# Seven block products for eight in the first product of a second MLP

## The chip, the cores and the metric

The kernel runs on one core of a Trainium2 chip (trn2). The metric is the device time of one execution in microseconds (us), as a median over runs. The engines are named as the profile names them: PE (TensorE matmul), PEld (its weight loads), DVE (VectorE), ACT (ScalarE), POOL (GpSimd), SP (SyncE, which starts the DMAs).

## What is computed

Causal attention with a window of 64 positions (4 batches, 8 heads, 576 positions, head size 64), then two MLPs on the 2304 tokens of width 512. All of it in float32:

```python
x = attn_out.transpose(0, 2, 1, 3).reshape(2304, 512)
h = x @ w_in                       # 512 -> 2048
x = (h * tanh(softplus(h))) @ w_out
h = x @ w_in2                      # 512 -> 1024: the first product of the second MLP
e = exp(h - h.max(-1)); sm = e / (e.sum(-1) + 1e-9)
solu = h * sm
ln = (solu - solu.mean(-1)) / sqrt(solu.var(-1) + 1e-6) * g_ln
return ln @ w_out2                 # 1024 -> 512
```

## The kernel before

Every float32 operand of a large product is split into a high half that PE takes exactly (rounded, type fp32r) and a low half (the value less the high half), and a product is three matmuls: high x high, high x low, low x high. `round_12` makes a high half, `rest` (L304) a low half; the engine is an argument.

The tokens go through attention and the first MLP in five groups of 512, 512, 512, 384 and 384. In the first MLP an iteration takes one of 16 slices of 128 hidden units: 12 matmuls into PSUM (`pe_m1`, L742), the activation on ACT (`act_m`, L752), its high half `g` (mostly ACT, L288) and low half (DVE, L308), then 8 matmuls on the high half (`pe_m2`, L776) and 4 on the low half (`pe_m2l`, L787), added up in four banks over the 16 slices. Attention of the next group runs beside it. The result goes to DRAM (`x2d`).

The second MLP takes the tokens in 18 tiles of 128. For each tile: `b_load` (L850) fetches it, transposed, as four blocks of 128 of the 512 inputs; `b_split` (ACT, L855) and `b_rest` (POOL, L860) make its halves; `b_m3` (L870) is 24 matmuls (4 blocks x 3 terms x 2 halves of the 1024 outputs) into the two banks of `h`; `b_max` (DVE, L877), `b_exp` (ACT, L883), `b_stat` (DVE, L889 on: h times exp, then mean and variance), `b_var` (POOL), `b_z` (DVE, L910 and L911) make the normed row; `b_tr` (L918) is 8 transposes; `b_hi` (ACT) and `b_lo` (DVE) split it; `b_m4` (L943) is 24 matmuls of the second product, `b_out` and `b_store` bring it out.

The weights arrive as float64 bits and are made float32 on the chip, piece by piece (`convert`): `c_up`, `c_low` (ACT or POOL), `c_bits`, `c_sign` (DVE), then `c_hi` and `c_lo`. Finished halves lie in buffers of two rings of four, `w1` and `w2`; the four pieces of `w_in2` (called w3) and those of `w_out2` (w4) take the buffers of the first MLP's weights as these come free, in its last group.

Nothing of this is in a fixed order in the code. Each piece of work is a `step` with its engines and assumed costs (`COSTS`), what it follows, what buffers it uses, and a due time; `Schedule.run` lays the steps out one by one, on each engine the one with the earliest due time among those that could start about now, and calls the functions in that order. So the order of instructions on each engine is what the tables of due times (`PRE_AT`, `ATT_AT`, `B_AT` and others, L50 to L69) make of it, and the engines then keep that order. Where a step of PE in the first part would stand idle for over 0.8 us by these costs, `bridge` (L518) fills the gap with small matmuls on zeros.

Of the kernel before, what the change touches and what calls it, by code (L numbers as in the profile page):

```python
# [24 lines left out]
P = 128  # L25
# [30 lines left out]
B_AT = (9.587, 37.912, -19.559, -30.209, 0.809, 34.651, 64.819, 43.703)

CONV_PRIO = (43.465, 59.161, 15.699, 11.465, 9.993, -9.387)
Q_LEAD = 1.101
V_LEAD = -62.18  # L60
G_AT = 1.058
K0_LATER = -88.806
FIRST_AT = (-161.938, -95.173, -8.712)
W_STEP = 0.88
M4_LATER = -28.799
BESIDE_AT = ((12.83, 25.285), (5.132, 29.901), (-14.786, 53.657), (-18.384, 60.677), (13.158, 1.338))
BESIDE_PE = 15.387
PATIENCE = 0.35
SLACK = 7.152  # L69
# [127 lines left out]
def attention_moe_solu(  # L197
# [624 lines left out]
    with tc.manual_schedule():  # L822
# [9 lines left out]
        def open_b():  # L832
            tctx.close()
            B["x"] = ctx.enter_context(tc.tile_pool(name="bx", bufs=2, side="right", reuse_waits="tile"))
            B["s"] = ctx.enter_context(tc.tile_pool(name="bs", bufs=4, side="right", reuse_waits="tile"))
            B["h0"] = ctx.enter_context(tc.tile_pool(name="pb_h0", bufs=1, space=PSUM, side="right", reuse_waits="tile"))
            B["mhalf"] = B["s"].tile([P, 1], F32, name="mhalf", bufs=1)
            nc.vector.memset(B["mhalf"], -0.5)

        def open_b2():  # L840
# [4 lines left out]
            B["h1"] = ctx.enter_context(tc.tile_pool(name="pb_h1", bufs=1, space=PSUM, reuse_waits="tile"))  # L845

        def b_load(t):
            j, o = tile_of[t]
            xr[t] = B["x"].tile([P, KD, P], F32, tag="xr", name="xr", bufs=1)
            nc.sync.dma_start(out=xr[t], in_=x2d[j][:, :, o:o + P])  # L850

        def b_split(t):
            r = xr.pop(t)
            xs[t] = B["x"].tile([P, 2, KD, P], F32R, tag="xs", name="xs", bufs=2)
            nc.scalar.activation(out=xs[t][:, 0], in_=r, func=ACTF.Copy)  # L855
            xr[t] = r

        def b_rest(t):
            r = xr.pop(t)
            nc.gpsimd.tensor_tensor(out=xs[t][:, 1], in0=r, in1=xs[t][:, 0].bitcast(F32), op=ALU.subtract)  # L860

        def b_m3(t):
            h2[t] = B["h" + str(t % 2)].tile([P, 2, 512], F32, tag="h2", name="h2")
            x = xs.pop(t)
            assert all(("w3", c, k) in split_done for c in range(2) for k in range(KD))

            terms = [(k, a, b) for k in range(KD) for a, b in ((0, 1), (0, 0), (1, 0))]
            for idx, (k, a, b) in enumerate(terms):
                for c in range(2):
# [387 lines left out]
```

## Time and profile before

| | |
|---|---|
| median of 3 runs | 704.94 us (704.12 to 705.28) |
| profiled execution | 706.97 us |
| its span (first to last instruction) | 705.1 us |
| busy share: PE, DVE, ACT, POOL | 99%, 54%, 44%, 8% |
| mean granted clock of PE, as a share of 2.4 GHz | 0.998 |

The span is what the trace covers; the profiled execution is 1.9 us longer than it, and 2.0 us above the median. Ends of matmuls are modelled in the records, each reaching into the next, so the spacing of matmuls is read from starts. An engine that is idle costs nothing unless the chain of waits runs through it.

### The profile page before, as it was taken

The page shows a single profiled execution, that of the slowest core. Times are in us where ns is not written, and L with a number is a line of the kernel's source. Part 1 is how long each engine was busy: PE and PEld are TensorE (multiplying, and loading weights), DVE is VectorE, ACT ScalarE, POOL GpSimd, SP SyncE. Part 2 cuts the span into 40 slices and gives each one's busy share as a digit, 9 for nine tenths or more (in the row PEclk, how much of TensorE's full clock was granted, in tenths as well). Part 3 has the DMA queues.
Part 4 walks back from the last instruction along what each step waited for, and adds up shares of the span by engine and source line. Part 5 has one row for each costly group of instructions (what it writes and reads, how often), then busy time and mean ns, then how long its engine had stood idle before and what let it go on. Part 6 is the DMA issues. An engine that isn't in the chain of part 4 may idle for free.

```text
span 705.1 us, 10722 instructions
## 1 busy us (share of the span) xinstructions
PE 695.4 (99%) x4429; PEld 597.2 (85%) x4429; DVE 382.0 (54%) x559; ACT 312.1 (44%) x536; POOL 56.9 (8%) x80
## 2 busy tenths in 40 slices
PE   9989999999999999999999999999999999999997
PEld 7779888888888888878899999999888888888886
DVE  4988776775662121656614114666766556565550
ACT  5769977475442222454534325663322222222231
POOL 2111000010000000000001100001122212111000
PEclk9999999999999999999999999999999999999999
DMA  8747355846213030323150105330111111110011
GB/s 288 296 156 293 121 178 179 278 160 219 90 46 106 0 119 31 119 91 120 31 165 1 31 1 165 120 119 32 44 59 46 46 45 46 46 45 31 16 45 46
DMA packets 37856, 71.74 MB, mean 102 GB/s; under 512 B 2864, under 2 KB 15152, under 8 KB 37808
## 3 DMA queue, kind: packets, MB, share of 16 engines
q1 hardware_dynamic: 37808, 71.06, 29.9%
q8 instruction: 35, 0.57, 0.3%
q14 instruction: 13, 0.11, 0.0%
HBM read 59.51 MB, written 11.53 MB: 101 GB/s over the span
## 4 chain that ended last, share of the span: by engine, by line
PE 94%; DVE 3%; DMA 2%; ACT 1%; issue 0%; SPq 0%; ACTq 0%
PE ps_h L742 27%; PE x L776 18%; PE h L870 14%; PE po L943 14%; PE x L787 9%; PE ps_o L696 2%; PE pt L918 2%; PE ps_t L659 2%; PE ps_s L564 2%; PE ps_w L516 1%; DMA st<-w_in 1%; DMA room_kv<-v 1%; PE ps_s L546 1%; DVE w L308 0%; DVE g L308 0%; DVE su L633 0%
## 5 line engine op out<-in xcount | busy, mean ns | idle before, releaser
L742 PE MATMUL ps_h<-xt,w 128*128 128x512 f32 (+2 forms) x1008 | 212.3, 361 | 0.3 <-ACT mc L752 0.2
L742 PEld LDWEIGHTS ps_h<-xt,w 128*128 128x128 f32 x1008 | 178.1, 189 | 22.9 <-issue 1.0
L776 PE MATMUL x<-g,w 128*128 128x512 f32 (+2 forms) x672 | 147.9, 362 | 0.0
L776 PEld LDWEIGHTS x<-g,w 128*128 128x128 f32 x672 | 118.1, 188 | 14.6 <-issue 0.9
L308 DVE SCALAR_TENSOR_TENSOR g<-mc,g 128x512 fp32r<-128x512 f32 (+2 forms) x84 | 53.2, 635 | 117.5 <-ACT g L288 117.0
L870 PE MATMUL h<-w,xs 128*128 128x512 f32 x432 | 104.0, 396 | 0.0
L943 PE MATMUL po<-w,lz 128*128 128x512 f32 x432 | 102.8, 394 | 0.0
L870 PEld LDWEIGHTS h<-w,xs 128*128 128x128 f32 x432 | 80.9, 188 | 19.0
L943 PEld LDWEIGHTS po<-w,lz 128*128 128x128 f32 x432 | 80.0, 188 | 16.3
L288 ACT ACTIVATE g<-mc 128x512 fp32r<-128x512 f32 (+2 forms) x70 | 39.8, 572 | 97.9 <-PE x L787 97.5
L787 PE MATMUL x<-g,w 128*128 128x512 f32 (+2 forms) x336 | 81.2, 363 | 0.0
L752 ACT ACTIVATE mc<-ps_h 128x512 f32<-128x512 f32 (+2 forms) x84 | 44.6, 535 | 78.1 <-PE ps_h L742 64.3
L787 PEld LDWEIGHTS x<-g,w 128*128 128x128 f32 x336 | 59.1, 188 | 7.1 <-issue 0.5
L924 ACT ACTIVATE lz<-pt 128x512 fp32r<-128x512 f32 x36 | 19.6, 596 | 63.2 <-PE po L943 49.5
L877 DVE TENSOR_REDUCE nm<-h 128x1 f32<-128x1024 f32 x18 | 22.0, 1224 | 45.8 <-PE h L870 45.8
L647 POOL TENSOR_TENSOR s<-s,rs 128x1024 f32<-128x1024 f32 x7 | 13.5, 1934 | 348.8 <-DVE rs L641 342.8
L368 DVE SCALAR_TENSOR_TENSOR st<-st 128x1024 uint32<-128x1024 uint32 x22 | 26.9, 1224 | 25.5 <-ACT st L360 25.5
L855 ACT ACTIVATE xs<-xr 128x512 fp32r<-128x512 f32 x18 | 11.4, 632 | 59.7 <-issue 32.2
L860 POOL TENSOR_TENSOR xs<-xr,xs 128x512 fp32r<-128x512 f32 x18 | 23.3, 1293 | 167.6 <-ACT xs L855 167.6
L889 DVE TENSOR_TENSOR y<-h,y 128x1024 f32<-128x1024 f32 x18 | 22.0, 1223 | 14.5 <-ACT y L883 14.5
L928 DVE TENSOR_TENSOR lz<-pt,lz 128x512 fp32r<-128x512 f32 x36 | 23.3, 686 | 12.2 <-ACT lz L924 11.0
L353 ACT ACTIVATE st<-st 128x1024 f32<-128x1024 f32 x22 | 25.3, 1149 | 9.5 <-DMA st<-w_in 6.4
(102 smaller groups left out, 651.7 us busy)
## 6 DMA issues: line engine op xcount, KB each, us to landing
qk<-qk SPq DMA_DIRECT2D x32, 512.0 KB, 5.0
st<-w_out SPq DMA_DIRECT2D x12, 1024.0 KB, 5.0
st<-w_in SPq DMA_DIRECT2D x10, 1024.0 KB, 5.7
v<-v SPq DMA_DIRECT2D x32, 256.0 KB, 3.4
xr<-x2d SPq DMA_DIRECT2D x18, 256.0 KB, 3.1
out<-o SPq DMA_DIRECT2D x18, 256.0 KB, 2.0
x2d<-xs SPq DMA_DIRECT2D x12, 256.0 KB, 2.9
part<-xs SPq DMA_DIRECT2D x8, 256.0 KB, 3.2
```

Of the source, the lines that this page charges most:

```text
L288: nc.scalar.activation(out=hi, in_=x, func=ACTF.Copy, scale=1.0 if g is None else g)
L308: nc.vector.scalar_tensor_tensor(out=lo, in0=x, scalar=1.0 if g is None else g, in1=hi.bitcast(F32), op0=ALU.mult, op1=ALU.subtract)
L353: nc.scalar.activation(out=w, in_=w, func=ACTF.Copy, scale=2.0**-112)
L368: nc.vector.scalar_tensor_tensor(out=lw, in0=uw, scalar=3, in1=lw, op0=ALU.logical_shift_left, op1=ALU.bitwise_or)
L742: nc.tensor.matmul(out=ps[:, :n], lhsT=w[:, a, k, fs], rhs=x[:, b, k, a0:a1], start=(idx == 0), stop=(idx == len(terms) - 1),)
L752: nc.scalar.activation(out=c[:, :n], in_=ht.pop(i)[:, :n], func=ACTF.Mish)
L776: nc.tensor.matmul(out=acc[j][m][:, a0:a1], lhsT=w[:, a, f % 4, m * P:(m + 1) * P], rhs=g[:, 0, :n], start=(i in opens and a == 0), stop=F ...
L787: nc.tensor.matmul(out=acc[j][m][:, a0:a1], lhsT=w[:, 0, f % 4, m * P:(m + 1) * P], rhs=g[:, 1, :n], start=False, stop=i in closes,)
L860: nc.gpsimd.tensor_tensor(out=xs[t][:, 1], in0=r, in1=xs[t][:, 0].bitcast(F32), op=ALU.subtract)
L870: nc.tensor.matmul(out=h2[t][:, c, :], lhsT=x[:, a, k, :], rhs=wt["w3", c][:, b, k, :], start=(idx == 0), stop=(idx == len(terms) - 1),)
L928: nc.vector.tensor_tensor(out=lt[t][:, 1, fs], in0=pst[t][:, fs], in1=lt[t][:, 0, fs].bitcast(F32), op=ALU.subtract)
L943: nc.tensor.matmul(out=po[t], lhsT=lz[:, a, f, :], rhs=wt["w4", f // 4][:, b, f % 4, :], start=(c == 0 and idx == 0), stop=(c == 2 and idx ...
```

## The change

Tiles 2u and 2u+1 become a pair. Its rows are two blocks, the 512 inputs two halves, the 1024 outputs two halves, so the first product of a pair is a 2x2 product of blocks, and Strassen's scheme (in Winograd's form) makes it from seven block products. A block product is 6 matmuls (2 blocks of 128 inputs x 3 terms), so a pair is 42 matmuls where it was 48.

- The weights: the four pieces B11, B12, B22, B21 of w3 are loaded in that order, and four combinations T1 to T4 of them are made (`t_sum`, POOL or DVE) and split into halves too; B12 itself is not needed in halves. They lie in four buffers where there were two; w4 moves from ring `w1` to ring `w2`.
- The tokens: `b_sum` makes four sums of the pair's blocks on POOL, 256 values each (in the tile `raw` for the first pair, in `s_b` for the others); `b_hi_a`, `b_lo_a` split the three plain blocks that are used, `b_hi_s`, `b_lo_s` the four sums.
- The products P0 to P6 (`b_p`) go into four banks: P0, then on top of it P3, then P6 in bank 0; P1, then P4 in bank 1; P2 in bank 2; P5 in bank 3. What stands in a bank after P0, P3, P6 and P1 is copied to SBUF (`b_v`, ACT or DVE) before the next product is added.
- Four closing sums on DVE (`b_c`; C00, C01 of the first tile, C10, C11 of the second) add a bank and a copy, or for C11 two copies, write the row of h to SBUF and give its maximum. `b_max` then only takes the larger of two numbers. `b_exp` and `b_stat` read h from SBUF, not from PSUM.
- All tables of due times have new numbers; two of them are in the diff.

```diff
-B_AT = (9.587, 37.912, -19.559, -30.209, 0.809, 34.651, 64.819, 43.703)
+B_AT = (-28.972, 56.758, -35.729, -40.521, -29.935, -24.796, 36.091, 98.229)
+P_AT = (-3.0, -2.5, -2.0, 0.0, 0.1, 0.2)
...
+    T_OF = {1: (("st", 1), ("st", 0)), 2: (("st", 3), ("t", 1)), 3: (("st", 3), ("st", 1)), 4: (("st", 2), ("t", 2))}
+    def t_sum(e, i):
+        if "raw" not in room:
+            room["raw"] = x_p.tile([P, 4, 1024], F32, tag="xt", name="raw")
+        a, b = (w3_st[n] if of == "st" else w3_t[n] for of, n in T_OF[i])
+        w3_t[i] = room["raw"][:, i - 1]
+        eng = nc.gpsimd if e == "pool" else nc.vector
+        eng.tensor_tensor(out=w3_t[i], in0=a, in1=b, op=ALU.subtract)
...
-        def b_m3(t):
...
-            terms = [(k, a, b) for k in range(KD) for a, b in ((0, 1), (0, 0), (1, 0))]
-            for idx, (k, a, b) in enumerate(terms):
-                for c in range(2):
-                    nc.tensor.matmul(
-                        out=h2[t][:, c, :], lhsT=x[:, a, k, :], rhs=wt["w3", c][:, b, k, :],
-                        start=(idx == 0), stop=(idx == len(terms) - 1),
-                    )
+        def b_sum(e, u):
...
+            for i, a, b, op in (
+                (0, a21, a22, ALU.add), (1, s[:, 0], a11, ALU.subtract), (2, a11, a21, ALU.subtract),
+                (3, a12, s[:, 1], ALU.subtract),
+            ):
+                nc.gpsimd.tensor_tensor(out=s[:, i], in0=a, in1=b, op=op)
+        PRODUCTS = ((0, 0, 0, True), (3, 3, 1, True), (1, 1, 2, True), (4, 4, 0, False), (6, 2, 1, False),
+                    (2, 6, 3, True), (5, 5, 0, False))
+        def b_p(u, i):
+            ix, iw, bank, first = PRODUCTS[i]
...
+            terms = [(k, a, w) for k in range(2) for a, w in ((0, wlo), (0, whi), (1, whi))]
+            for n, (k, a, w) in enumerate(terms):
+                nc.tensor.matmul(
+                    out=ps, lhsT=x[:, a, ix, k, :], rhs=w[:, k, :], start=first and n == 0, stop=n == len(terms) - 1,
+                    skip_group_check=not first,
+                )
+        def b_c(u, i, c):
...
+            bank, v = ((2, 0), (1, 1), (3, 2), (None, 2))[2 * i + c]
+            nc.vector.tensor_tensor_reduce(
+                out=hs[t][:, c], in0=B["v"][:, 3] if bank is None else banks[u, bank], in1=B["v"][:, v], scale=1.0,
+                scalar=-3.0e38, op0=ALU.add, op1=ALU.max, accum_out=mx[t][:, c:c + 1],
+            )
...
-            nc.vector.tensor_reduce(out=nm, in_=h2[t], axis=AX.XY, op=ALU.max, negate=True)
+            nc.vector.tensor_scalar(
+                out=nm, in0=m[:, :1], scalar1=m[:, 1:], scalar2=-1.0, op0=ALU.max, op1=ALU.mult
+            )
```

The order of instructions, as the scheduler leaves it. First PE in the middle of the second MLP, before: the last matmuls of one tile's first product (`h2`, on w3's two halves `w30`, `w31`), the transposes of another tile (`pt`), the second product of a third (`po`), and the next tile.

```order
L870 MATMUL h2_4950<-w30_3887,xs_4848 128x512
L870 MATMUL h2_4950<-w31_4038,xs_4848 128x512
L918 MATMUL pt_4986<-ident_70,y_4824 128x128 x8
L943 MATMUL po_4999<-w40_4177,lz_4878 128x512 x8
L943 MATMUL po_4999<-w41_4309,lz_4878 128x512 x8
L943 MATMUL po_4999<-w40_4177,lz_4878 128x512 x4
L943 MATMUL po_4999<-w41_4309,lz_4878 128x512 x4
L870 MATMUL h2_5043<-w30_3887,xs_4902 128x512
```

And now: one pair's products (`pb`, one number for each bank; `xs` is the pair's operand), a tile's transposes behind the second of them, and a tile's second product at the end.

```order
L943 MATMUL pb_4987<-w30_3897,xs_4796 128x512 x6
L943 MATMUL pb_5000<-w31_4044,xs_4796 128x512 x6
L1010 MATMUL pt_5012<-ident_70,y_4846 128x128 x8
L943 MATMUL pb_5023<-w30_3897,xs_4796 128x512 x6
L943 MATMUL pb_4987<-w32_4196,xs_4796 128x512 x6
L943 MATMUL pb_5000<-w31_4044,xs_4796 128x512 x6
L943 MATMUL pb_5062<-w33_4149,xs_4796 128x512 x6
L943 MATMUL pb_4987<-w32_4196,xs_4796 128x512 x6
L1035 MATMUL po_5083<-w40_4243,lz_4842 128x512 x8
L1035 MATMUL po_5083<-w41_4380,lz_4842 128x512 x8
L1035 MATMUL po_5083<-w40_4243,lz_4842 128x512 x4
L1035 MATMUL po_5083<-w41_4380,lz_4842 128x512 x4
```

The first product of two tiles stands together, with the transposes and the second product of one tile beside it; the second products that are left over come at the end of the kernel.

PE where the first MLP ends: the last matmul on a low half of g, then the products of the first two pairs.

```order
L829 MATMUL x2_3_3950<-g_4378,w23_1719 128x384
L943 MATMUL pb_4420<-w30_3897,xs_3849 128x512 x6
L943 MATMUL pb_4433<-w31_4044,xs_3849 128x512 x6
L943 MATMUL pb_4420<-w32_4196,xs_3849 128x512 x6
L943 MATMUL pb_4433<-w31_4044,xs_3849 128x512 x6
L943 MATMUL pb_4420<-w32_4196,xs_3849 128x512 x6
L943 MATMUL pb_4494<-w30_3897,xs_3849 128x512 x6
L943 MATMUL pb_4503<-w33_4149,xs_3849 128x512 x6
L943 MATMUL pb_4517<-w30_3897,xs_4483 128x512 x6
L943 MATMUL pb_4534<-w31_4044,xs_4483 128x512 x6
L943 MATMUL pb_4553<-w30_3897,xs_4483 128x512 x6
L943 MATMUL pb_4517<-w32_4196,xs_4483 128x512 x6
```

Thirteen products (the one more is P5 of the second pair) stand ahead of the first transposes; before, the first product of tile 0 stood among the last matmuls of the first MLP.

POOL over the end of the first MLP, before: the last two products of attention, then low halves of tiles (`xs`) and the first variance.

```order
L647 TENSOR_TENSOR s_1674<-s_1674,rs_1765 128x1024
L647 TENSOR_TENSOR s_3449<-s_3449,rs_3527 128x1024
L860 TENSOR_TENSOR xs_3644<-xr_3626,xs_3644 128x512
L860 TENSOR_TENSOR xs_3689<-xr_3676,xs_3689 128x512
L860 TENSOR_TENSOR xs_4371<-xr_3712,xs_4371 128x512
L904 TENSOR_SCALAR va_4409<-va_4409 128x1
L905 TENSOR_TENSOR va_4409<-va_4409,mhalf_3624 128x1
```

And now, in the same place (`w30` to `w33` are the four buffers of w3, `raw` the combinations T1 to T4 and later the first pair's sums).

```order
L311 TENSOR_TENSOR w30_3897<-st_1765,w30_3897 128x1024
L410 TENSOR_TENSOR raw_3739<-st_3925,raw_3739 128x1024
L311 TENSOR_TENSOR w31_4044<-raw_3739,w31_4044 128x1024
L410 TENSOR_TENSOR raw_3739<-st_4046,raw_3739 128x1024
L311 TENSOR_TENSOR w33_4149<-raw_3739,w33_4149 128x1024
L311 TENSOR_TENSOR w32_4196<-raw_3739,w32_4196 128x1024
L913 TENSOR_TENSOR raw_3739<-xr_3815 128x256
L913 TENSOR_TENSOR raw_3739<-raw_3739,xr_3815 128x256
```

Six operations on 1024 values per partition come in front of the first pair's sums (two more of these and the low half of the sums follow). Over the whole program PE has 125 filler matmuls on zeros where it had 113, and the copies, the low halves of the sums and the low halves of the plain blocks are shared out: 34 copies on ACT and 2 on DVE, 6 low halves of sums on POOL and 3 on DVE, 8 of plain blocks on POOL and 1 on DVE.

## Rows read from the trace of the kernel before

**Rows 1.** The page, part 1: busy time, share of the span, instructions of each engine.

```profile
PE 695.4 (99%) x4429; PEld 597.2 (85%) x4429; DVE 382.0 (54%) x559; ACT 312.1 (44%) x536; POOL 56.9 (8%) x80
```

**Rows 2.** The page, part 4: the chain that ended last, by line.

```profile
PE ps_h L742 27%; PE x L776 18%; PE h L870 14%; PE po L943 14%; PE x L787 9%; PE ps_o L696 2%; PE pt L918 2%; PE ps_t L659 2%; PE ps_s L564 2%; PE ps_w L516 1%; DMA st<-w_in 1%; DMA room_kv<-v 1%; PE ps_s L546 1%; DVE w L308 0%; DVE g L308 0%; DVE su L633 0%
```

**Rows 3.** Stretches: length, busy PE, PEld, DVE, ACT, POOL (instructions), clock, DMA share, GB/s.

```profile
40.00:44.00 4.00, 4.00 (x35) 3.83 (x28) 3.96 (x5) 0.38 (x1) 0.00 (x0) 0.61 0.61 203
...
430.00:477.60 47.60, 47.40 (x273) 47.08 (x272) 27.45 (x34) 29.77 (x43) 0.00 (x0) 1.00 0.40 138
...
477.60:503.80 26.20, 26.20 (x130) 22.83 (x130) 14.53 (x27) 8.05 (x15) 2.08 (x3) 1.00 0.12 41
...
551.64:575.56 23.92, 23.92 (x113) 19.71 (x112) 13.32 (x24) 6.83 (x12) 4.18 (x7) 1.00 0.14 45
```

**Rows 4.** Timeline of PE, second MLP: start us, us, engine, line, operation.

```profile
551.64 5.76 PE L870 MATMUL h<-w,xs 128*128 128x512 f32 x24
...
557.25 1.03 PE L918 MATMUL pt<-ident,y 128*128 128x128 f32 x8
...
558.04 5.73 PE L943 MATMUL po<-w,lz 128*128 128x512 f32 x24
...
563.60 2.73 PE L870 MATMUL h<-w,xs 128*128 128x512 f32 x11
```

**Rows 5.** Timeline of PE, first MLP, 512-token group.

```profile
266.11 2.88 PE L742 MATMUL ps_h<-xt,w 128*128 128x512 f32 x12
...
268.83 1.98 PE L776 MATMUL x<-g,w 128*128 128x512 f32 x8
```

**Rows 6.** Timeline of PE, the last stretch.

```profile
688.36 12.97 PE L943 MATMUL po<-w,lz 128*128 128x512 f32 x56
```

**Rows 7.** Groups by line and form: busy us, mean ns | idle before.

```profile
L877 DVE TENSOR_REDUCE nm<-h 128x1 f32<-128x1024 f32 x18 | 22.0, 1224 | 45.8 <-PE h L870 45.8
...
L892 DVE BATCH_NORM_STATS2 st<-y 128x6 f32<-128x512 f32 x36 | 23.2, 686 | 0.6
...
L860 POOL TENSOR_TENSOR xs<-xr,xs 128x512 fp32r<-128x512 f32 x18 | 23.3, 1293 | 167.6 <-ACT xs L855 167.6
...
L647 POOL TENSOR_TENSOR s<-s,rs 128x1024 f32<-128x1024 f32 x7 | 13.5, 1934 | 348.8 <-DVE rs L641 342.8 <-ACT xt L300 6.0
...
L353 ACT ACTIVATE st<-st 128x1024 f32<-128x1024 f32 x22 | 25.3, 1149 | 9.5 <-DMA st<-w_in 6.4 <-DMA st<-w_out 3.1
...
L300 ACT ACTIVATE s<-ps_t 128x512 f32<-128x512 f32 x32 | 17.3, 595 | 8.3 <-PE ps_t L659 8.3
...
L911 DVE TENSOR_SCALAR y<-y,mv,c 128x1024 f32<-128x1024 f32 x18 | 14.6, 813 | 0.7
```

**Rows 8.** Timeline of all engines, first pairs of attention.

```profile
36.22 2.41 DVE L308 SCALAR_TENSOR_TENSOR g<-mc,g 128x256 fp32r<-128x256 f32 x2
...
36.45 1.90 POOL L647 TENSOR_TENSOR s<-s,rs 128x1024 f32<-128x1024 f32 x1 [6.05 <-ACT xt L300]
...
39.29 1.10 PE L564 MATMUL ps_s<-qk 64*64 64x128 f32 x32 [1.89 <-DVE xt L718]
...
40.32 2.50 PE L742 MATMUL ps_h<-xt,w 128*128 128x256 f32 x12
```

**Rows 9.** Timeline, second MLP, 503.5 to 512.5.

```profile
504.83 1.29 POOL L860 TENSOR_TENSOR xs<-xr,xs 128x512 fp32r<-128x512 f32 x1
...
504.97 1.16 DVE L910 TENSOR_TENSOR c<-va,r 128x1 f32<-128x1 f32 x1
```

**Rows 10.** Groups by line and form, window 550 to 600.

```profile
L910 DVE TENSOR_TENSOR c<-va,r 128x1 f32<-128x1 f32 x5 | 0.8, 159 | 5.0 <-POOL va L905 5.0
```

**Rows 11.** Timeline, end of the first MLP.

```profile
470.10 0.56 DVE L308 SCALAR_TENSOR_TENSOR g<-mc,g 128x384 fp32r<-128x384 f32 x1 [1.13 <-ACT g L288]
...
470.67 0.85 PE L787 MATMUL x<-g,w 128*128 128x384 f32 x4
```

**Rows 12.** Timeline of PE, before the first product of the first MLP.

```profile
26.99 1.92 PE L516 MATMUL ps_h<-warm 128*128 128x256 bf16 x16
```

More of the change, by code (lines that the diff above doesn't have):

```diff
@@ L396, in c_lo @@
     def c_lo(e, p):
-        split_done.update((p["name"], p["c"] if p["name"] == "w3" else 0, p["f"] + i) for i in range(p["k"]))
+        if p["name"] == "w3":
+            hi, lo = w3_halves((0, None, 1, 2)[p["w3"]])
+            rest(e, lo, p["wf"].rearrange("p (k f) -> p k f", k=2), hi)
+            return
+        split_done.update((p["name"], 0, p["f"] + i) for i in range(p["k"]))
         hi, lo, w = c_halves(p)
@@ L844, in open_b2 @@
             B["o"] = ctx.enter_context(tc.tile_pool(name="pb_o", bufs=2, space=PSUM, reuse_waits="tile"))
-            B["h1"] = ctx.enter_context(tc.tile_pool(name="pb_h1", bufs=1, space=PSUM, reuse_waits="tile"))
+            B["p1"] = ctx.enter_context(tc.tile_pool(name="pb_1", bufs=1, space=PSUM, reuse_waits="tile"))
+        sums, ops, banks, mx, hs = {}, {}, {}, {}, {}
         def b_load(t):
+            u, i = divmod(t, 2)
             j, o = tile_of[t]
-            xr[t] = B["x"].tile([P, KD, P], F32, tag="xr", name="xr", bufs=1)
@@ L850, in b_load @@
[L850 to L860, printed above, removed]
[L862 to L873 removed]
+            if i == 0:
+                xr[u] = B["x"].tile([P, 2, KD, P], F32, tag="xr", name="xr")
@@ new lines, in b_load @@
+            nc.sync.dma_start(out=xr[u][:, i], in_=x2d[j][:, :, o:o + P])
+        def b_sum(e, u):
+            x = xr[u]
+            if u == 0:
+                s = room["raw"][:, 0].rearrange("p (i k t) -> p i k t", i=4, k=2)
+            else:
+                s = B["z"].tile([P, 4, 2, P], F32, tag="s", name="s_b", bufs=1)
+            sums[u] = s
+            a11, a12, a21, a22 = x[:, 0, :2], x[:, 0, 2:], x[:, 1, :2], x[:, 1, 2:]
+            for i, a, b, op in (
[3 more added lines that the diff above has]
+                nc.gpsimd.tensor_tensor(out=s[:, i], in0=a, in1=b, op=op)
@@ new lines, in b_hi_s, with b_lo_s @@
+        def b_hi_s(e, u):
+            round_12(e, ops[u][:, 0, 3:], sums[u])
+        def b_lo_s(e, u):
+            rest(e, ops[u][:, 1, 3:], sums[u], ops[u][:, 0, 3:])
+        PRODUCTS = ((0, 0, 0, True), (3, 3, 1, True), (1, 1, 2, True), (4, 4, 0, False), (6, 2, 1, False),
+                    (2, 6, 3, True), (5, 5, 0, False))
+        def b_p(u, i):
+            ix, iw, bank, first = PRODUCTS[i]
+            if first:
+                banks[u, bank] = B["p0" if bank < 2 else "p1"].tile([P, 512], F32, tag=f"p{bank}", name="pb")
+            ps, x = banks[u, bank], ops[u]
+            whi, wlo = w3_halves(iw)
+            terms = [(k, a, w) for k in range(2) for a, w in ((0, wlo), (0, whi), (1, whi))]
[4 more added lines that the diff above has]
+                )
@@ new lines, in b_v @@
+        def b_v(e, u, n, bank):
+            copy(e, B["v"][:, n], banks[u, bank])
+        def b_c(u, i, c):
+            t = 2 * u + i
+            if c == 0:
+                hs[t] = B["z"].tile([P, 2, 512], F32, tag="h", name="h_b", bufs=4)
+                mx[t] = B["s"].tile([P, 2], F32, tag="mx", name="mx")
+            bank, v = ((2, 0), (1, 1), (3, 2), (None, 2))[2 * i + c]
[3 more added lines that the diff above has]
+            )
@@ L975, in convert @@
             key = nm, p["c"]
-            fresh = key not in whole
+            fresh = nm != "w3" and key not in whole
             if fresh:
@@ L1167, in attention_moe_solu @@
         )
[L1168 to L1170 removed]
+        UB = 11.1 / 4.16
         all_w4 = [s for (nm, _, _), s in split_of.items() if nm == "w4"]
[L1172 to L1179 removed]
+        vb = [Buf("bv%d" % i) for i in range(4)]
```

194 lines of the change are left out of this document (153 added, 41 removed).

## The prediction

> **What bounds the kernel now.** I read the page first: PE is busy for 99% of the span, DVE for 54%, ACT for 44%, POOL for 8% [rows 1]. The chain of waits says the same by time: it runs almost wholly through PE, and the lines of matmuls follow each other in it [rows 2]. A PE that is busy throughout can still be waiting for small things, so I then read the table of stretches. From 430 us to the end of the first MLP PE is busy for 47.40 of 47.60 us at full clock, and in the second MLP for all of it [rows 3]. The one place that falls out is near 40 us, where the mean granted clock is 0.61 [rows 3]. So time leaves the second MLP only if PE's own work gets shorter, and it comes back wherever PE is made to wait. Last I read the timeline of PE there: a token tile is 24 matmuls of the first product, 8 transposes and 24 of the second, and the next tile starts 563.60 - 551.64 = 11.96 us later [rows 4].
>
> **The removed matmuls.** Before, the first product is 18 x 24 = 432 matmuls. Now the order of PE has 9 pairs x 7 products x 6 = 378 rows of pb; so the change does what it says, and 54 are gone. Before, 24 of them took from 551.64 to 557.25, or 0.234 us each [rows 4], which makes 432 x 0.234 = 101.0 us. The price of one of the new matmuls isn't in the trace; I bound it by others of the same width. Twelve in a row into one bank took 268.83 - 266.11 = 2.72 us, 0.227 each [rows 5]; the 56 that close the kernel took (12.97 - 0.39) / 55 = 0.229, a last one being 0.39 long in the records [rows 6]. The old ones wrote two banks by turns, the new ones fill one bank six times, as those two do; I take 0.2275, so 378 x 0.2275 = 86.0 us and **-15.0 us**. The ends are -15.3 (at 0.2267) and -12.6 (at 0.234).
>
> **What is added on the other engines, per pair of tiles.** Before, two tiles cost DVE 13.3 us, ACT 6.8 and POOL 4.2 in 23.9 us of PE [rows 3].
> - DVE: two row maxima of 1.22 go [rows 7]. Four closing sums of 512 with a maximum come. Such an operation isn't in the trace: from below it is 0.69, a 128x512 pass over one row's values, from above 1.22, a pass of twice the length [rows 7]; the nearer is the first, and with a small operation of 0.16 behind it [rows 10] I take 0.85. With two small maxima and, in three pairs of nine, a low half of 1024 values (1.22 by the maximum's row, 0.4 on the mean) DVE has 13.3 - 2.4 + 3.4 + 0.3 + 0.4 = 15.0 us.
> - ACT: four copies of a bank at 0.6 and the rounding of the sums at 1.15 [rows 7] come, about 10 in all.
> - POOL: four sums of 256 values (half of 1.29, 0.65 each) and 768 values of low halves come for two old passes of 1.29 [rows 7]: 4.2 - 2.6 + 2.6 + 1.9 = 6.1, and in six pairs of nine the low half of the sums, 2.6, so 7.8 on the mean.
> - PE has 9.6 + 2 x (0.79 + 5.56) = 22.3 [rows 4]. None of the others reaches that, so I cost them at nothing while PE has work queued; the order lets m4 of a tile run only two tiles behind its transposes, which leaves DVE most of a period for each.
>
> **The start of the second MLP: +1.2.** This is the place without a queue: 13 products stand ahead of the first transposes. Counted from the last matmul of the first MLP, product P1 of the second pair is the ninth and would start at 8 x 1.37 = 10.9 us. The low half it reads is made by POOL after ACT has copied the bank of P6 (fifth in PE's order, so 6.9 + 0.2 + 0.6 = 7.7) and rounded the sums (1.15, so 8.9 with the handover): two passes of 1.29 end at 11.5, and PE, which stands in order, starts at 11.7 instead of 10.9: +0.8. Tile 0's chain through four closing sums, exp, the product, the statistics and z ends within 0.2 of the moment when PE reaches its transposes, and tile 1's likewise: +0.4. At the upper price of a closing sum, five of them in front of z add 2.7 us. Ends 0 and +4.
>
> **The end of the first MLP: +1.3.** Before, POOL does nothing from 430 to 477.6 [rows 3]. Now it makes there six passes of 1024 values, four sums and another such pass: 7 x 2 x 1.29 + 2.6 = 20.7 us (13.5 + 2.6 by the row of 1.93 [rows 7]). What that does to DVE the trace shows twice. Two short DVE passes took 2.41 us while a POOL pass of 1.90 ran [rows 8]; an operation on one value per partition, 0.16 us elsewhere [rows 10], took 1.16 while POOL's 1.29 ran [rows 9]. And the low halves of g, which DVE makes with both operands in SBUF, are due at once: one ended at 470.66 and PE's matmuls on it began at 470.67 [rows 11]. I take one wait on the path, of half a POOL pass, 1.3: what PE once loses there it need not lose again, since DVE works ahead by as much. Ends 0 and, if all eight hit, +10.4.
>
> **The order at the start: +1.4.** The tables of due times are new, so everything is reordered. PE's order has 125 filler matmuls where there were 113; 16 take 1.92 us [rows 12], 12 more 1.4, and fillers stand where PE has nothing to do. From below: before, PE waited 1.89 us for DVE at 39.29 [rows 8], and then worked at clock 0.61 for 4 us [rows 3], which is 4 x 0.39 = 1.6 us lost (its next 12 matmuls took 2.50 us [rows 8]); if the new order has no such gap, -3.5. From above another such gap, +3.5.
>
> **The sum.** -15.0 + 1.2 + 1.3 + 1.4 = -11.1 us. The profiled execution took 706.97 us (705.1 span and 1.9 around it), so it would take 695.9; the median of the runs, 704.94, lies 2.0 below it, hence **693.8 us**.
>
> **Rivals.**
> - *The matmuls stay at 0.234.* If the cause is not the two banks but the operands, the saving is 12.6: 696.2 us. Against it are all three other groups of this width.
> - *The start gets better.* No gap and no half clock near 40 us, no longer idle: 693.8 - 1.4 - 3.5 = 689 us.
> - *POOL holds up DVE at every pass at the end of the first MLP.* Eight waits of 1.3 instead of one: 702.9 us. For it speaks the zero slack of [rows 11]; against it, that one such wait of PE leaves DVE ahead for the ones behind it.
> - *DVE becomes the bound of the second MLP, and the kernel slower.* The product h x exp was read from PSUM and now reads two operands in SBUF; so do C11, the low halves and c. If every POOL pass keeps DVE waiting for its whole length, as in [rows 9], and a closing sum costs 1.38, DVE needs 15.0 + 4 x 0.53 + 7.8 = 24.9 us for each pair. It decides from 22.3 + 11.1 / 9 = 23.5 us per pair on; at 24.9 it is 9 x 2.6 = 23 us on top, 717 us. Against it: DVE is free when most of POOL's passes start, and POOL would have to hit it each time. The Trainium skill, "SBUF — State Buffer", section "Who interferes with whom", says that a VectorE instruction with two inputs in SBUF and a GpSimd instruction that reads SBUF exclude each other for a whole instruction, and that the order of issue decides who waits; by that rule this case and the one above are live. The trace agrees where it shows the pair: 1.16 us for 0.16 [rows 9, 10].
> - *Nothing to be seen.* The two losses of the last cases together with the old matmul price eat the saving: 705 us.
>
> **Chances.** Forecast 0.56, own range 691 to 696; matmuls at 0.234 0.13; better start 0.15; POOL at every pass 0.10; DVE the bound 0.04; nothing 0.02. A measurement of this kernel tells about 0.2%, 1.4 us, from no change. Faster: 0.56 + 0.13 + 0.15 + 0.10 = 0.94; same 0.02; slower 0.04. The range from 689 to 699 takes in the forecast, the matmul price and most of the better start, and leaves out POOL at every pass, DVE as the bound, no change, and the edges of the others, some 0.2.
>
> **What would show it.** Right: a spacing of the pb matmuls near 0.227; a wait of PE of 1 us or less before the ninth product; no idle PE from there to the end; DVE near 15 us of busy time per pair. Wrong: low halves of g of 2 us and more beside POOL passes, with PE waiting behind each; the m4 matmuls or transposes waiting for DVE in the middle of the second MLP; a second stretch at a clock near 0.6; or the first product of the first MLP starting over 2 us later than at 29 us.

## The result, and the profile after

The changed kernel takes 708.38 us (median of 17 runs, 705.78 to 713.52), the kernel before 704.29 (17 runs, 703.31 to 706.57). The ratio is 1.006, with an interval of 1.0045 to 1.0075: slower by some 4 us, where 693.8 was forecast. The profiled execution of the changed kernel took 709.72 us, its span is 707.9 and its mean clock 0.994. The five runs with a mean clock of 1.000 took 705.8 to 707.9, so even these are above the median of the kernel before.

The page, part 1, and the start of the chain (against [rows 1, 2]):

```profile
PE 687.6 (97%) x4387; PEld 588.4 (83%) x4387; DVE 421.9 (60%) x644; ACT 339.6 (48%) x576; POOL 122.9 (17%) x127
...
PE 83%; DVE 10%; POOL 2%; DMA 2%; ACT 2%; issue 1%; ACTq 0%; DVEq 0%; POOLq 0%
```

PE is busy for 7.8 us less than before, 687.6 for 695.4, and the span is 2.8 us longer: work left PE, and more waiting came back. A tenth of the chain now runs through DVE. The table of stretches (length, busy time of PE, PEld, DVE, ACT, POOL with instructions, clock, DMA share, GB/s) says where, against [rows 3]:

```profile
40.00:44.00 4.00, 2.50 (x45) 2.25 (x46) 3.96 (x5) 1.13 (x1) 0.00 (x0) 1.00 0.44 140
440.00:492.00 52.00, 47.88 (x268) 45.96 (x267) 42.02 (x39) 28.99 (x40) 23.05 (x10) 1.00 0.33 112
492.00:563.00 71.00, 65.00 (x288) 52.51 (x287) 59.60 (x118) 35.56 (x61) 49.32 (x50) 0.95 0.18 56
519.10:522.50 3.40, 2.80 (x11) 2.64 (x12) 3.36 (x7) 0.82 (x2) 3.40 (x4) 0.51 0.00 0
...
608.00:630.50 22.50, 22.50 (x109) 18.78 (x108) 14.18 (x33) 7.97 (x15) 1.56 (x4) 1.00 0.07 24
```

Before, the same two stretches were:

```profile
440.00:492.00 52.00, 52.00 (x292) 50.82 (x291) 31.74 (x44) 30.21 (x46) 2.08 (x3) 1.00 0.25 86
492.00:563.00 71.00, 71.00 (x333) 58.18 (x332) 46.58 (x80) 20.53 (x37) 14.98 (x21) 1.00 0.16 53
```

PE stands idle in two places where it never did: 4.1 us at the end of the first MLP (440 to 492) and 6.0 us in the first part of the second (492 to 563), where a wait is also followed by a stretch at clock 0.51, the lower of the two levels, 1.2 GHz (a second one lies at 556.6). From 608 on it is busy throughout. Near 40 us the clock is 1.00 where it was 0.61, but PE is idle for 1.5 of the 4 us.

The products themselves did what was forecast, nearly. In the timeline of PE, 24 of them take 545.80 - 540.24 = 5.56 us, 0.232 each; all 378, by their starts outside of waits and half clock, 88.0 us for 101.1 before: 13.1 saved.

```profile
540.24 5.73 PE L943 MATMUL pb<-w,xs 128*128 128x512 f32 x24
...
545.80 5.60 PE L1035 MATMUL po<-w,lz 128*128 128x512 f32 x24
```

The view of PE's waits, 440 to 492 and then 492 to 563 (what waited, for what: us in total, times, longest):

```profile
PE ps_h L784 <- ACT mc L794: 3.3, 5, 1.4
PE x L818 <- DVE g L297: 0.8, 1, 0.8
...
PE pt L1010 <- DVE y L1003: 3.8, 2, 2.8
PE pt L1010 <- DVE nm L966: 2.1, 2, 1.8
```

So 4.1 and 5.9 us. (The expectations below count the same waits by the spacing of PE's starts, which gives 5.75 and 6.9; the measured waits below are always those of this view. The rows put down to `nm` are waits for the bank `pt`, which the low halves `lz` of the tile before leave free just then.) In the second MLP it is the transposes that wait, not the products. One of these waits in the timeline of all engines:

```profile
509.93 1.19 DVE L1003 TENSOR_SCALAR y<-y,mv,c 128x1024 f32<-128x1024 f32 x1
510.53 2.83 POOL L311 TENSOR_TENSOR xs<-s_b,xs 128x1024 fp32r<-128x1024 f32 x1
511.04 3.40 DVE L981 TENSOR_TENSOR y<-h_b,y 128x1024 f32<-128x1024 f32 x1
511.17 1.09 PE L1010 MATMUL pt<-ident,y 128*128 128x128 f32 x8 [0.93 <-DVE y L1003]
...
515.31 1.56 PE L943 MATMUL pb<-w,xs 128*128 128x512 f32 x6
...
517.64 0.58 DVE L1002 TENSOR_TENSOR c<-va,r 128x1 f32<-128x1 f32 x1
...
518.26 1.30 DVE L1003 TENSOR_SCALAR y<-y,mv,c 128x1024 f32<-128x1024 f32 x1
...
519.70 1.94 PE L1010 MATMUL pt<-ident,y 128*128 128x128 f32 x8 [2.83 <-DVE y L1003]
```

POOL begins a pass of 2.83 us; the product h x exp of tile 1, both of whose operands lie in SBUF, is issued half a microsecond later and takes 3.40 us, until POOL's pass is over and 1.1 us more. Tile 1's row is normed at 519.56, and PE, which has had only 20 matmuls between the two tiles' transposes, waits 2.83 us for it. It is not this pass alone. DVE's groups in 492 to 563 (busy us, mean ns | idle before):

```profile
L981 DVE TENSOR_TENSOR y<-h_b,y 128x1024 f32<-128x1024 f32 x7 | 11.6, 1664 | 3.1 <-ACT y L975 3.1
...
L958 DVE CUSTOM_DVE_ANT_0 h_b<-pb,v_b 128x512 f32<-128x512 f32 x13 | 8.8, 683 | 2.7 <-PE pb L943 2.7
L1003 DVE TENSOR_SCALAR y<-y,mv,c 128x1024 f32<-128x1024 f32 x6 | 7.3, 1216 | 0.2
...
L958 DVE CUSTOM_DVE_ANT_0 h_b<-v_b 128x512 f32<-128x512 f32 x4 | 4.8, 1209 | 0.0
L1002 DVE TENSOR_TENSOR c<-va,r 128x1 f32<-128x1 f32 x6 | 4.6, 772 | 1.0 <-POOL va L997 1.0
```

The closing sums that read a bank (`pb`) take 683 ns each, the one of two copies in SBUF 1209 (687 in run 7 below); an operation on one value per partition takes 772 instead of 159 [rows 10], the normed row 1216 instead of 813 [rows 7]. The end of the first MLP shows the same in another place:

```profile
454.72 2.90 POOL L410 TENSOR_TENSOR raw<-st,raw 128x1024 f32<-128x1024 f32 x1 [8.40 <-DVE st L379]
455.35 3.36 DVE L313 SCALAR_TENSOR_TENSOR w<-st,w 128x1024 fp32r<-128x1024 f32 x1
...
458.63 0.55 DVE L313 SCALAR_TENSOR_TENSOR g<-mc,g 128x384 fp32r<-128x384 f32 x1
...
459.21 0.49 ACT L794 ACTIVATE mc<-ps_h 128x384 f32<-128x384 f32 x1 [0.50 <-DVE g L313]
459.75 2.38 PE L784 MATMUL ps_h<-xt,w 128*128 128x384 f32 x12 [1.43 <-ACT mc L794]
```

A low half of w3 takes 3.36 us beside POOL's pass, the low half of g behind it is late, ACT cannot fill the buffer `mc`, and PE waits 1.43 us for a free bank.

### The profile page after: what moved, and what is told of

Its sections match the earlier page's. It is cut to its first block, busy times and chain, and to the rows that moved or that the text cites. A ratio compares the mean times of both kernels' runs of the same rounds, so it can differ in the third digit from the quotient of the medians.

```text
span 707.9 us, 10782 instructions
## 1 busy us (share of the span) xinstructions
PE 687.6 (97%) x4387; PEld 588.4 (83%) x4387; DVE 421.9 (60%) x644; ACT 339.6 (48%) x576; POOL 122.9 (17%) x127
## 4 chain that ended last, share of the span: by engine, by line
PE 83%; DVE 10%; POOL 2%; DMA 2%; ACT 2%; issue 1%; ACTq 0%; DVEq 0%; POOLq 0%
PE ps_h L784 25%; PE x L818 17%; PE po L1035 12%; PE pb L943 9%; PE x L829 8%; PE ps_o L738 2%; PE ps_s L606 2%; PE pt L1010 2%; PE ps_t L701 2%; DMA st<-w_in 2%; DVE y L981 1%; PE ps_w L558 1%; DVE st L984 1%; POOL raw L913 1%; DVE h_b L958 1%
## 5 line engine op out<-in xcount | busy, mean ns | idle before, releaser
L313 DVE SCALAR_TENSOR_TENSOR g<-mc,g 128x512 fp32r<-128x512 f32 (+2 forms) x84 | 57.2, 684 | 102.5 <-ACT g L293 101.5
L943 PE MATMUL pb<-w,xs 128*128 128x512 f32 x378 | 92.7, 400 | 0.1
L293 ACT ACTIVATE g<-mc 128x512 fp32r<-128x512 f32 (+2 forms) x66 | 38.1, 579 | 110.2 <-PE x L829 109.9
L943 PEld LDWEIGHTS pb<-w,xs 128*128 128x128 f32 x378 | 71.5, 191 | 16.2 <-DVE mx L958 0.5
L689 POOL TENSOR_TENSOR s<-s,rs 128x1024 f32<-128x1024 f32 x8 | 15.2, 1900 | 368.3 <-DVE rs L683 231.4
L305 ACT ACTIVATE v_b<-pb 128x512 f32<-128x512 f32 x34 | 20.4, 601 | 47.8 <-PE pb L943 39.5
L981 DVE TENSOR_TENSOR y<-h_b,y 128x1024 f32<-128x1024 f32 x18 | 25.9, 1437 | 19.6 <-ACT y L975 19.6
L975 ACT ACTIVATE y<-h_b,nm 128x1024 f32<-128x1024 f32 x18 | 20.7, 1152 | 19.5 <-PE pt L1010 17.8
L760 DVE TENSOR_TENSOR xt<-ps_o,xt 128x512 fp32r<-128x512 f32 (+1 forms) x20 | 12.5, 631 | 27.4 <-ACT xt L305 27.4
```

The costliest lines, as they stand in the source:

```text
L293: nc.scalar.activation(out=hi, in_=x, func=ACTF.Copy, scale=1.0 if g is None else g)
L313: nc.vector.scalar_tensor_tensor(out=lo, in0=x, scalar=1.0 if g is None else g, in1=hi.bitcast(F32), op0=ALU.mult, op1=ALU.subtract)
L943: nc.tensor.matmul(out=ps, lhsT=x[:, a, ix, k, :], rhs=w[:, k, :], start=first and n == 0, stop=n == len(terms) - 1, skip_group_check=not ...
L981: nc.vector.tensor_tensor(out=y, in0=h2.pop(t), in1=y, op=ALU.mult)
```

## The experiments

The theories: **A**, mutual exclusion: while GpSimd reads two operands in SBUF, VectorE's passes that need the same way into SBUF stand still. **B**: VectorE simply has too much to do. **C** and **D**, formed after the first runs: GpSimd's queue is too long, for the variances of a tile (C) or for the operands of the products (D). Every ratio is against runs of the kernel before on the same chip.

**1 to 3. GpSimd that reads nothing, in the second MLP, at the end of the first, in both.** The edit, here for the low halves; the sums and T are done alike (the first run for pairs 1 to 8, the second for w3 and pair 0, the third for all):

```diff
+    def fill_in(out, n, *ins, op=ALU.subtract):
+        one = lambda t: t[(slice(None),) + (slice(0, 1),) * (len(t.shape) - 1)]
+        nc.gpsimd.tensor_tensor(out=one(out), in0=one(ins[0]), in1=one(ins[1]), op=op)
+        for _ in range(n):
+            nc.gpsimd.memset(out.bitcast(F32), 0.0)
...
-        if e == "pool":
+        if e == "pool" and fill:
+            fill_in(lo, fill, x, hi.bitcast(F32))
+        elif e == "pool":
```

> In the changed kernel, every low half and every sum that GpSimd makes for the pairs after the first is left out: in its place a subtraction of one column, which keeps the wait for the same data, and three fills of the same tile with zeros, which read nothing (so part of h is missing). The order of instructions stays. Theory A: the PE waits of the second MLP (6.9 us between 492 and 563 us in the changed kernel, and two stretches at half clock behind them) come from GpSimd and VectorE keeping each other out of SBUF, since GpSimd reads two operands there. Then the product h x exp goes back from 1.66 us on the mean in that stretch to about 1.22, the operation on one value per partition (L1002) from 0.77 to 0.16, the PE waits there fall below 2 us, no half clock is left, and the time is 698 to 702 us against about 708.4 of the changed kernel. Theory B: VectorE has simply too much to do in front of the first transposes, whatever GpSimd does: the waits stay above 5 us and the time above 706.

> The same replacement, but only at the end of the first MLP: the combinations T1 to T4 and the low halves of w3 that GpSimd makes, and its sums and low halves for the first pair (so part of w3 and of the first pair is missing); the pairs after it are as in the changed kernel. Theory A (mutual exclusion): the low halves of g and w there take their own 0.56 and 1.22 us, and the PE waits between 440 and 492 us fall from 5.75 us to below 2; the time is about 704 us (4 less than the changed kernel), with the waits of the second MLP as they were. Theory B (the order puts the long VectorE passes on w3 ahead of the halves of g): PE still waits over 4 us there, time about 708.

> Both replacements at once. Theory A: the two gains add up, about 694 to 698 us, which is what the fewer matmuls alone were forecast to give. Theory B: 706 to 708 us, no gain. If the waits go in one place only, the time lies between, by the wait that is left.

The second run went as theory A has it: 703.85 us (ratio 0.9995, 0.9975 to 1.0014), 4.5 below the changed kernel. GpSimd is busy there for longer than in the changed kernel (26.08 us for 23.05), the low halves of w3 on VectorE take 1226 ns instead of 3281, and of the 4.1 us of PE's waits 1.2 are left (the stretch, then the waits):

```profile
440.00:492.00 52.00, 50.79 (x284) 49.25 (x284) 30.81 (x40) 31.71 (x45) 26.08 (x42) 1.00 0.39 127
...
PE ps_h L794 <- ACT mc L804: 1.2, 1, 1.2
```

The first did not: 711.17 us (1.010, 1.0074 to 1.0126), slower still, with 8.2 us of waits in the second MLP. The third, with both, took 705.94 (1.004, 1.0024 to 1.0056), the gain of the one and the loss of the other. In the first run's stretch of 492 to 563 us the exclusion is gone (the one-value operation takes 158 ns again), but DVE now stands idle for 12.8 us in front of it, because three fills are longer than the pass they replace, and POOL is busy for 57.57 us where it was for 49.32:

```profile
492.00:563.00 71.00, 62.90 (x287) 50.48 (x286) 47.94 (x112) 35.55 (x60) 57.57 (x145) 0.98 0.18 56
```

```profile
L1013 DVE TENSOR_TENSOR c<-va,r 128x1 f32<-128x1 f32 x6 | 0.9, 158 | 12.8 <-POOL va L1008 12.8
```

So the run had exchanged one cause for another, and did not tell A from C. The next ones had to part them.

**4 to 6. Short fills; the variance on VectorE; both that and the long fills.**

```diff
-            nc.gpsimd.tensor_scalar(out=va, in0=va, scalar1=1e-6, scalar2=None, op0=ALU.add)
-            nc.gpsimd.tensor_tensor(out=va, in0=va, in1=B["mhalf"], op=ALU.pow)
+            nc.vector.tensor_scalar(out=va, in0=va, scalar1=1e-6, scalar2=None, op0=ALU.add)
+            nc.vector.reciprocal(out=va, in_=va)
```

> As the first of the runs (no GpSimd reads for the pairs after the first; part of h is missing), but with one fill for each pass where that one had three, so GpSimd is busy for less than in the changed kernel instead of for longer (one fill of 1024 values took 0.95 us, one of 256 took 0.33). Theory C, new: GpSimd runs its instructions in order, and the small operations on a tile's variance (L996, L997) stand in its queue behind the passes for the pairs; VectorE waits for them with its next operation (in the first run it was idle for 12.8 us for that between 492 and 563 us), and PE for VectorE. By theory C, and by theory A (mutual exclusion) too, the waits of PE there fall from 6.9 to below 2.5 us and the time to 699 to 703 us. By theory B (VectorE has too much to do in any case) the waits stay above 5 us and the time above 706.

> GpSimd's passes are as in the changed kernel; the two small operations on a tile's variance are done by VectorE, at the same places of the program, as an addition and a reciprocal (so the root is left out, and the rows are scaled wrongly). VectorE no longer waits for GpSimd's queue in the middle of a tile, but its passes on two operands in SBUF are still kept waiting by GpSimd's. Theory C alone (the queue): waits of PE between 492 and 563 us below 2.5 us, time 699 to 703. Theory A alone (mutual exclusion): waits above 6 us, time 707 to 710. Both together: waits of 3 to 6 us, time 703 to 707.

> The variance on VectorE as in the run before, and GpSimd's passes for the later pairs replaced by three fills each, which read nothing and are longer than the passes (GpSimd was busy for 58 of 71 us with them in the first run, 47 in the changed kernel). Neither the queue nor the exclusion can hold VectorE. Theories A and C: waits of PE below 2.5 us between 492 and 563 us, time 699 to 703. What this run has less than the run before is the exclusion alone. Theory D: GpSimd is simply late with the operands of the products, which PE then waits for at pb rows: the waits stay above 5 us, and stand in front of products and not of transposes.

Short fills: 699.52 us (0.9928, 0.9911 to 0.9945), and PE is busy throughout from 492 to 563:

```profile
492.00:563.00 71.00, 71.00 (x331) 58.33 (x330) 53.61 (x131) 39.11 (x69) 35.68 (x94) 1.00 0.21 63
```

Theory B is out for the changed kernel: DVE's own work there leaves PE no wait. The variance on VectorE alone gained nothing: 710.14 us (1.0087, 1.0063 to 1.0111), at the upper end of theory A's range, with 7.3 us of waits, most of them in front of the same transposes. Theory C is not what the changed kernel suffers from.

```profile
PE pt L1010 <- DVE y L1003: 3.4, 2, 3.2
PE pt L1010 <- DVE nm L966: 3.1, 2, 1.6
PE pb L943 <- DVE mx L958: 0.8, 1, 0.8
```

The sixth run missed what both theories expected: 708.76 us (1.0061, 1.0046 to 1.0076). POOL, busy for 59.04 of 71 us (49.32 in the changed kernel, where the expectation has 47), is late with the sums; ACT's rounding of them holds up ACT's queue, and PE waits in front of transposes. That is a form of theory D, and it comes from the fills being long:

```profile
536.64 1.06 ACT L293 ACTIVATE xs<-s_b 128x1024 fp32r<-128x1024 f32 x1 [5.94 <-POOL s_b L313]
...
540.14 1.09 PE L1021 MATMUL pt<-ident,y 128*128 128x128 f32 x4 [4.70 <-DVE nm L977]
```

**7. Fills as long as the passes.** The first edit with two fills instead of three.

> As the first run, with two fills for each pass of GpSimd, so that GpSimd is busy about as long as its passes take without a VectorE beside them (2.2 us for 1024 values, 0.86 for a sum of 256, by 0.95 and 0.33 us for a fill), and reads next to nothing; the variances stay on GpSimd (part of h is missing). Theory A (mutual exclusion): VectorE's operations take their own times and the waits of PE between 492 and 563 us fall from 6.9 to below 2 us; time 699 to 702, as with the short fills. Theories C and D (the length of GpSimd's queue, for the variances or for the operands of the products): the waits stay above 5 us, time above 705.

702.23 us (0.9968, 0.9955 to 0.9981), 6.2 below the changed kernel. POOL is busy for 51.41 us, a little longer than in the changed kernel, and the waits of 492 to 563 are 1.3 us instead of 5.9:

```profile
492.00:563.00 71.00, 69.74 (x327) 57.03 (x326) 55.29 (x132) 38.95 (x66) 51.41 (x129) 1.00 0.18 56
```

```profile
PE pt L1021 <- DVE nm L977: 1.1, 1, 1.1
PE pt L1021 <- DVE y L1014: 0.2, 1, 0.2
```

With POOL as long in use, only its reads left out, the waits go. Theory A holds in the second MLP too.

**8, 9, 10 and 12. The passes on VectorE.** In 8 the table of costs gives these steps no other engine, and the order is made anew; 9 and 12 also have other due times, and each a longer assumed cost for one step of the statistics or the normed row (not in the diff); 10 keeps the changed kernel's order and only issues the passes on VectorE.

```diff
-    "t": {"pool": 2.64, "dve": 1.22}, ... "t_lo": {"dve": 1.22, "pool": 2.64},
-    "sum": {"pool": 2.8}, ... "lo_a": {"pool": 2.05, "dve": 1.15},
-    "lo_s": {"pool": 2.64, "dve": 1.22},
+    "t": {"dve": 1.22}, ... "t_lo": {"dve": 1.22},
+    "sum": {"dve": 1.5}, ... "lo_a": {"dve": 1.15},
+    "lo_s": {"dve": 1.22},
...
-                nc.gpsimd.tensor_tensor(out=s[:, i], in0=a, in1=b, op=op)
+                nc.vector.tensor_tensor(out=s[:, i], in0=a, in1=b, op=op)
```

> Nothing is left out. The combinations T, their low halves, the sums of the pairs and the low halves of the operands may run on VectorE only (the planner makes a new order from that; all due times are as in the change). VectorE takes 1.2 us where GpSimd took 2.6, and nothing excludes it any more: by the single rows it gets some 10 us more work at the end of the first MLP and 2.6 for each pair, about 19 in the first 71 us of the second MLP, and loses the 11 us by which its own passes were stretched there. Theory A: the waits at the end of the first MLP go (5.75 to below 1.5), those of the second MLP fall to 2 to 6 us; time 692 to 700. Theory B (VectorE has too much to do): it is busy throughout from 492 to 563 us, the waits grow beyond 10 us, time 706 or more.

> As the run before, and the due times of the second MLP's steps (B_AT, P_AT, T_AT, M4_LATER) are other ones, by which the first products of a pair, the statistics of its tiles and the second products alternate more evenly. Theory A with enough room on VectorE: no waits from 440 us to the end but for some 2 us, time 688 to 694. If the order of the steps is no part of the cause, the time is that of the run before, within 1.5 us.

> The same passes on VectorE, but in the order of the changed kernel: each is issued at the very place where GpSimd's stood in the program, so PE's and ScalarE's orders are those of the change. Theory A: the waits at the end of the first MLP go from 5.75 to below 2 us, and those between 492 and 563 us from 6.9 to 2 to 6; time 698 to 704. Theory B: above 706, with VectorE busy throughout.

> The passes on VectorE only, and a second set of due times for the second MLP, meant to take away the last waits (0.9 us in front of the second transposes, and short ones in front of the last second products). Theory: no wait of over 0.5 us from 440 us to the end, time 694 to 696 us, some 1 us below the first such kernel (696.1). A wait that comes back in the first 60 us of the second MLP would give 697 or more.

In the same order (10) the time is 704.71 us (1.0006, 0.9991 to 1.0022), just above A's range and below B's. The waits at the end of the first MLP are gone; those of the second MLP are larger, 8.8 us where A had 2 to 6, and here theory B is right: DVE is busy for 64.20 of 71 us with work of its own.

```profile
492.00:563.00 71.00, 62.20 (x280) 49.63 (x279) 64.20 (x154) 32.12 (x55) 9.69 (x14) 0.98 0.15 45
```

In the new order (8) 700.90 us (0.9951, 0.9935 to 0.9966), a little above A's range. One wait is left, of a product, and in the profiled execution the clock is 0.50 from 499.8 to 506.6, around it: the low half of the next pair's sums stands in DVE's queue behind a tile's statistics, until 501.4.

```profile
501.44 0.79 PE L943 MATMUL pb<-w,xs 128*128 128x512 f32 x1 [4.28 <-DVE xs L313]
```

Run 9 takes 696.14 us (0.9882, 0.9862 to 0.9902): one wait of 0.7 us is left, as expected, but the time is 2 us above the range given. It is 4.8 below run 8, so with nearly the same work on VectorE (706 and 710 instructions) another order is worth that much. Run 12, with the second set, takes 695.40 (0.9879, 0.985 to 0.9908), as expected, some 9 us below the kernel before; its longest wait is 0.5 us. These two are the best of the study, the same within what four runs tell. PE is busy for all of 440 to 492 in run 12, and after it:

```profile
492.00:563.00 71.00, 70.03 (x330) 57.48 (x329) 59.35 (x139) 34.06 (x58) 6.23 (x12) 1.00 0.15 49
```

**11. Another order.** Every pass may run on the engines that the change allows. Not in the diff below are two other due times and an assumed 1.5 us for the normed row instead of 0.92. The order is new, and with it the planner's choice of engines: of the sums' low halves between 492 and 563 us four are now on VectorE, where none was, and POOL is busy there for 45.45 us instead of 49.32.

```diff
-B_AT = (-28.972, 56.758, -35.729, -40.521, -29.935, -24.796, 36.091, 98.229)
-P_AT = (-3.0, -2.5, -2.0, 0.0, 0.1, 0.2)
+B_AT = (-14.151, -30.340, 33.552, 24.254, 15.283, -47.419, 45.759, 39.986)
+P_AT = (-7.599, 7.646, -1.197, 6.007, -11.030, 10.942)
...
-            sa = step(dict(dve=3.4), o[2], b_stat, t, after=[ex], new=[st], uses=[h, y, su, st])
+            sa = step(dict(dve=4.2), o[2], b_stat, t, after=[ex], new=[st], uses=[h, y, su, st])
```

> Every pass stays where the change may put it, on GpSimd too; only the due times of the second MLP's steps are other ones, and the planner is told longer VectorE steps for the statistics (4.2 for 3.4) and the normed row (1.5 for 0.92), as they take beside GpSimd. If the mutual exclusion makes PE wait only because the order asks for the operands of the next pairs and the rows of the first tiles at once, the waits of the second MLP fall from 6.9 to below 3 us with another order, those at the end of the first MLP stay at 5 to 7, and the time is 698 to 703 us. If the exclusion costs the waits in any order, they stay above 5 us in the second MLP too, and the time is 705 or more.

The waits went as the first reading has it, the time did not: 706.36 us (1.0029, 1.0015 to 1.0042), 2 below the changed kernel. The waits of the second MLP are 0.7 us instead of 5.9, though h x exp takes 1691 ns on the mean there; between the first two tiles' transposes PE now has 56 matmuls where it had 20. At the end of the first MLP 5.2 us are left (4.1 in the changed kernel), with two stretches at half clock behind them: the clock is 0.93 over these 52 us, which costs some 3.4 us more. The expected time had counted none, and the mean clock is 0.988 to 0.993 in all nine runs.

```profile
440.00:492.00 52.00, 46.78 (x245) 45.05 (x244) 41.13 (x35) 27.11 (x38) 21.52 (x10) 0.93 0.31 112
...
PE ps_h L784 <- ACT mc L794: 5.2, 4, 2.5
...
PE pb L943 <- ACT v_b L305: 0.7, 1, 0.7
```

## Why the prediction was wrong

- **The removed matmuls, -15.0: 13.1 saved.** Inside the ends of 12.6 and 15.3, but nearer to the rival's price: 0.232 us each, not 0.2275. The new matmuls fill one bank six times, so the two banks were not what made the old ones dear; what does stays open.
- **The start of the second MLP, +1.2 with ends 0 and +4: this is the step that failed.** By the spacing of starts it cost 6.9 us of waits and 3.1 of half clock behind them, 10.0. The sum followed PE to its first transposes and tile 1's chain to z, and put POOL's passes into the lateness of the operands only, not into DVE's chain. The 0.8 us for a late operand did not come: the first 78 matmuls, 13 products, take 18.15 us without a wait. What came is DVE's chain. There, from the end of z of tile 0 (511.12) to that of tile 1 (519.56), DVE took 8.4 us; PE's work between the two transposes ends with six matmuls from 515.31 on, so at 516.7, 5.5 us after the start of tile 0's transposes at 511.17. Without POOL's passes DVE's part is 8.4 less 2.18 (y), 0.42 (c) and 0.49 (z), some 5.35: just even, as runs 4 and 7 then showed (no wait, 1.3 us in all).
- **The end of the first MLP, +1.3 with ends 0 and +10.4: 5.75.** Inside, but mis-sized: "what PE once loses there it need not lose again" doesn't hold: PE waits six times there, because one pass of DVE after the other meets one of POOL's (four on w3 and T took 3.2 to 3.5 us, 1.22 being their own). Run 2 (waits of 4.1 down to 1.2 us, time 4.5 us less) shows the cause. DVE's load by itself is not it: it is busy there for 42.02 of 52 us, and in run 10 for 39.42, without a wait of PE.
- **The order at the start, +1.4:** 0.5, by the 1701st matmul of the first MLP, near 431 us, up to which PE has done the same work in both kernels but for the 12 fillers. The half clock near 40 us is gone, and other waits and the fillers take up what it gave.
- **The rest of the second MLP, nothing:** right from 563 us on; before that, "DVE is free when most of POOL's passes start" does not hold: POOL is busy for 49.32 of 71 us, DVE for 59.60. A closing sum was cheaper than taken, 0.683 + 0.08 for 0.85, so the wrong term is not DVE's work.
- **The rivals.** "POOL holds up DVE at every pass" at the end of the first MLP came half true. The one on the other side named the right mechanism and the wrong place: not DVE's sum over all nine pairs (14.18 of 22.50 us in a late stretch), but the first pairs, where PE has little queued. With 0.04 for slower, it was taken as a matter of throughput; a chance for the exclusion on the first tiles' path alone was missing.
- **The account of the profiled executions:** -13.1 for the products, -0.8 for the second products' spacing, +0.5 at the start, +5.75 and +10.0, together +2.4; the spans differ by 2.8, and 0.4 stays unassigned. The medians differ by 4.1, since the profiled execution of the kernel before lies 2.7 above its median and that of the changed kernel 1.3 above its own. The 3.1 of half clock belong to the profiled execution; five of the 17 runs show a mean clock of 1.000, and so next to none of it.

What is shown: the reads of GpSimd's passes cause the waits (runs 2 and 7), another order, with some passes moved, keeps those of the second MLP from PE (run 11), and with the passes on VectorE and a third order the fewer matmuls are worth some 9 us by the medians (run 12), near the -11.1 of the sum. The Trainium skill, "SBUF — State Buffer", section "Who interferes with whom", says that VectorE with two inputs in SBUF is held up by a GpSimd instruction that reads there, not by one that only writes; runs 1 and 7 agree (the one-value operation takes 158 and 156 ns beside fills, 772 beside passes). What was not tried: another order with every pass kept on its engine, and a second buffer for `mc` or `pt`, which would lengthen PE's queue instead of shortening DVE's.

## What to carry to other kernels

Work that is put on GpSimd "because it is idle" is paid for by VectorE too, if both read two operands in SBUF, and in some passes of one operand too (see below): add its length to VectorE's chain wherever they can meet, and give it to VectorE if that does it in half the time. Ask for this not over a whole stage but at the place where the bounding engine's queue is shortest, the first tiles of a stage: there compare the time between two of its instructions that need the other engine with that engine's chain between them. When an experiment takes away a resource's use, keep its length: the first run, with fills longer than the passes, showed a new wait and nearly hid the cause.

## What was not expected of the hardware

A cast with a single input in SBUF was held up as long as a pass with two. The normed row, one input too, was held up as well: in all its six slow cases in the changed kernel it ended 0.54 to 0.55 us after the GpSimd instruction that was under way at its start or began with it. Behind a pass of 256 values, 0.74 us long, it so took 1.2 to 1.3 us; behind one of 512 values, in run 5, it took 1.7 to 1.8. The same cast takes 0.35 us elsewhere, the normed row 0.81. From the changed kernel's timeline, then from that of run 5:

```profile
458.79 2.63 POOL L311 TENSOR_TENSOR w<-raw,w 128x1024 fp32r<-128x1024 f32 x1 [1.17 <-ACT w L293]
459.10 2.53 DVE L297 CAST g<-mc 128x384 fp32r<-128x384 f32 x1
...
550.95 0.74 POOL L311 TENSOR_TENSOR xs<-xr,xs 128x256 fp32r<-128x256 f32 x1
551.04 1.20 DVE L1003 TENSOR_SCALAR y<-y,mv,c 128x1024 f32<-128x1024 f32 x1
```

```profile
533.06 1.31 POOL L311 TENSOR_TENSOR xs<-xr,xs 128x512 fp32r<-128x512 f32 x1
533.16 1.76 DVE L1003 TENSOR_SCALAR y<-y,mv,c 128x1024 f32<-128x1024 f32 x1
```

Fills, which only write, hold up the normed row too, though not the operation with two inputs: in run 7 it took 1.06 us behind a fill of 0.53, and again ended 0.54 us after it.

```profile
532.91 0.53 POOL L313 MEMSET xs<- 128x512 f32 x1
532.92 1.06 DVE L1014 TENSOR_SCALAR y<-y,mv,c 128x1024 f32<-128x1024 f32 x1
```

The Trainium skill, "SBUF — State Buffer", section "Who interferes with whom", says that casts and scalar operations can use both of VectorE's port pairs, of which GpSimd shares one, and that the one which comes second is then blocked fully; both rows agree. A sum of two rows of 512 with its maximum costs no more on VectorE than a plain pass of that length (683 ns beside the 686 of [rows 7], and 80 for reading the maximum).
